# Attention and MLP in one kernel: q and k loads in a fixed chain of alternating halves, with a new order of all engines

## The chip, the cores and the metric

The kernel runs on one core of a Trainium2 chip. The metric is the device time of one execution in microseconds. Three runs of the kernel before took 606.34, 609.26 and 610.11 us, median 609.26 us.

## The reference

Causal attention over 4 batches, 12 heads, 448 tokens and a head size of 64, and then a feed-forward layer (768 to 2048 to 768) on the 1792 tokens that come out, all in float32:

```python
scores = (1.0 / np.sqrt(D)) * np.matmul(q, k.transpose(0, 1, 3, 2))
scores = np.where(np.triu(np.ones((S, S), dtype=bool), k=1), -1e9, scores)
attn = np.exp(scores - np.max(scores, axis=-1, keepdims=True))
attn = attn / (np.sum(attn, axis=-1, keepdims=True) + 1e-09)
x = np.matmul(attn, v).transpose(0, 2, 1, 3).reshape(B * S, H * D)
h = x @ w_in
g = np.where(h >= 1, h, np.where(h <= -1, 0.0, (h + 1) ** 2 / 4.0))
out = g @ w_out
```

## The kernel before, in words

**The work.** Two heads of a batch make a pair; there are 24. For a pair, q and k (two heads each) are loaded into `sq`, and DVE turns each into `qs` with a stream transpose (L736). PE makes the scores `s` (L838, in four PSUM buffers, all of which one pair fills), DVE adds the mask and takes the row minimum `mn` (L857, one instruction per tile of 64 to 448 columns and one that reads the minimum), ACT takes the exponential `e` with its row sum `su` (L861), the sum's reciprocal comes from DVE (L872), and `e` is scaled by it on POOL, ACT or DVE (L770, L772, L773). PE transposes `e` into `t` (L786), ACT or DVE copies it to `pt` (L809, L814), and PE multiplies it with v (`vr`) into `t` (L886). The result goes to `x` as a high and a low part (L470 or L471, and L479).

The first layer (`h`, L612) runs between the pairs' steps: for one batch and one block of 128 of the 2048 columns, six blocks of x by three passes (high by high, high by low, low by high), 18 matmuls. There are 64 such groups and two `h` buffers. Behind each group: `r = relu(h/2 + 1/2)` on ACT (L622), `vv = max(h, r)` on DVE (L625), and the clipped product `r = min(r, 1) * vv`, which is one instruction on DVE (L631) or two on POOL (L628, L629). `r` is stored to DRAM. There are three `r` buffers and one `vv` buffer. The weights of the first layer come as 384 KB loads into `w` and are decoded into a high and a low part in steps: ACT (L499, a Prelu into `wn`), DVE twice (L502, L504), then a copy (L470, L471) and a subtraction (L479 on DVE, L480 on POOL). There are four `wn` buffers. The weights of the second layer are decoded in the same way, combined by subtractions of `wn` to seven blocks per pair of rows, and kept in DRAM (`w_scratch`); the second layer (L1002) runs after all pairs, from about 400 us on.

**What sets the order.** The kernel lists tasks with the instructions that do them, what they read and write, and for some the engines that may do them. The class `Plan` puts them in order: it runs through a model of the engines and takes the next task by a rank. The tuple `STEPS` holds numbers, each of which seeds one random change of ranks or of the preferred engine (`shake`); the tuple therefore decides the order on all engines and who does what where there is a choice. A task that is `behind` another may not be put ahead of it in that order, but does not wait for its end. On the chip each engine works off its own list, and waits where a semaphore says so. All loads are issued by SP (L462).

**The loads of q and k.** `prep_pair` makes them. Pair 0 has two DMAs per tensor. Of the other 23 pairs each tensor (46 in all) has four DMAs of 32 partitions by 864 numbers (108 KB): head i and half z of the rows go to the partitions from `64 * i + 32 * z` on. Only the first of the four is `behind` something: the first load of the tensor before. The other three may be put anywhere after that, among other loads too. The transpose on DVE reads all four.

In the code, a program's names for buffers are those above. [rows n] in the prediction names the group of rows printed ahead of it.

Of the kernel before, what the change touches and what calls it, by code (L numbers as in the profile page):

```python
# [49 lines left out]
class Plan:  # L50
# [24 lines left out]
    def task(self, alts, prio, reads=(), writes=(), after=(), behind=()):  # L75
        t = Task([(*a, False) if len(a) == 3 else a for a in alts], prio)
        for b, k in reads:
            w, rs = b.keys.setdefault(k, [None, []])
            if w is not None:
                t.deps.add(w)  # L80
            rs.append(t)
        for b, k in writes:
            w, rs = b.keys.setdefault(k, [None, []])
            if w is not None:
                t.deps.add(w)
            t.deps.update(r for r in rs if r is not t)
            b.keys[k] = [t, []]
        for b in {id(x): x for x, _ in (*reads, *writes)}.values():
            if not b.tasks and b.tag is not None:
                t.allocs.append(b)  # L90
            elif b.tasks and b.tag is not None:
                t.soft.add(b.tasks[0])
            b.tasks.append(t)
        t.deps.update(after)
        t.soft.update(behind)
        t.deps.discard(t)
        t.soft -= t.deps
        for d in t.deps | t.soft:
            d.next.append(t)
        t.no = len(self.tasks)  # L100
        self.tasks.append(t)
        return t
# [47 lines left out]
    def solve(self):  # L150
# [23 lines left out]
        return self.run()  # L174

    STEPS = (
# [9 lines left out]
    )  # L186

    def shake(self, seed):
# [142 lines left out]
def mm(n, m=128, rows=128, times=1, pair=False):  # L331


    return [(n, m, rows, pair)] * times


def dve(n, fast=False):
    return ((n / 2 if fast else n) + 62) / 960


def act(n, extra=0.0):
    return n / 1200 + 0.055 + extra
# [10 lines left out]
def dma(nbytes, rate=250.0):  # L353
    return nbytes / rate / 1000
# [3 lines left out]
def kernel(  # L358
# [10 lines left out]
    B, H, S, D = q.shape  # L369
# [11 lines left out]
    C = S // 32  # L381
# [11 lines left out]
    LIGHT = 1  # L393
# [64 lines left out]
    def buf(tag, shape, dtype=F32):  # L458
        return plan.buf(tag, lambda: pools[tag].tile(shape, dtype, tag=tag, name=tag))

    def dma_task(out_fn, in_fn, cost, issue, early=False, lat=1.6, **kw):
        alts = [("SP", issue, lambda: nc.sync.dma_start(out=out_fn(), in_=in_fn())),  # L462
                ("ACT", issue, lambda: nc.scalar.dma_start(out=out_fn(), in_=in_fn()))]
        t = task(alts if early else alts[:1], 0.0, **kw)
        t.moved, t.lat = cost, lat
        return t
# [63 lines left out]
    ROW = C * D - 32  # L530
# [158 lines left out]
    attn_tasks, g_tasks, loads = [], [], []  # L689
# [5 lines left out]
    def tokens(t):  # L695
        return t[:, :NJ * 2 * D].rearrange("p (j g d) -> p j g d", g=2, d=D)

    def prep_pair(b, p, prio):
        no = b * HP + p
        x = QS[b, p] = [head[2 + g] if no == 0 else buf("qs", [P, S]) for g in range(2)]  # L700
        nat = []
        for g in range(2):
            t = head[g] if no == 1 else buf("sq", [P, ROW])
            first = None
            for i in range(2):
                row = (q, k)[g][b, 2 * p + i]
                if no < LIGHT:
                    one = dma_task(lambda i=i, t=t: tokens(t)[:, :, i],
                                   lambda row=row: bass.AP(row.tensor, row.offset, [[D, P], [P * D, NJ], [1, D]]),
                                   dma(NJ * P * D * 4, 228.0), 0.5, lat=1.45, early=no == 0, writes=[(t, i)],  # L710
                                   behind=loads[-1:] if first is None else ())
                    first = first or one
                    continue
                for z in range(2):
                    a = 64 * i + 32 * z
                    one = dma_task(lambda a=a, t=t: t[a:a + 32],
                             lambda row=row, z=z: bass.AP(row.tensor, row.offset + 32 * z, [[C * D, 32], [1, ROW]]),
                             dma(32 * 2 * S * 4, 230.0), 0.465, lat=1.25, writes=[(t, 2 * i + z)], behind=loads[-1:] if first is None else ())
                    first = first or one
            loads.append(first)  # L720
            nat.append(t)
        for g, t in enumerate(nat):
            if no < LIGHT:
                tb = buf("h" if no in (1, 2) or (no, g) == (0, 0) else "t", [P, 512])

                def tr(t=t, tb=tb):
                    for j in range(NJ):
                        n = min(P, S - j * P)
                        nc.tensor.transpose(tb[:, j * P:j * P + n], tokens(t)[:n, j].rearrange("p g d -> p (g d)"), ident[:n, :n])

                task([("PE", mm(215, 110, P, NJ), tr)], prio, reads=[(t, 0), (t, 1)], writes=[(tb, 0)]).nom = at(no, "S", 6) - LEAD + 0.1 * g
                task([("ACT", act(S, 0.04), lambda g=g, tb=tb: nc.scalar.activation(out=x[g].tile, in_=tb[:, :S], func=ACTF.Copy)),
                      ("DVE", dve(S), lambda g=g, tb=tb: nc.vector.tensor_copy(out=x[g].tile, in_=tb[:, :S]))],
                     prio, reads=[(tb, 0)], writes=[(x[g], 0)])
                continue
            task([("DVE", 0.81, lambda g=g, t=t: nc.vector.transpose(  # L736
                out=x[g].tile.rearrange("p (r c) -> p c r", c=C),
                in_=bands(t[:, :32])))],
                prio, reads=[(t, n) for n in range(4)], writes=[(x[g], 0)])
# [341 lines left out]
```

## Time and profile before

| | |
|---|---|
| runs | 606.34, 609.26, 610.11 us (median 609.26) |
| profiled execution | 608.45 us |
| its span | 606.7 us (1.75 us lie around it) |
| mean granted TensorE clock | 0.997 |
| PE busy | 588.1 us (97% of the span) |
| DVE, ACT, POOL busy | 454.0, 318.0, 147.5 us (75, 52, 24%) |

The profile is one execution. PE is the matrix engine, DVE the vector engine, ACT the scalar engine, POOL is GpSimd, SP issues the DMAs. A row of a timeline gives the start and the duration in us, the engine, the line of the kernel, the operation, what it writes and reads, the tile and the count; a bracket gives how long the engine stood idle before it, and what ended that. The granted clock is 1.00 at full speed (2.4 GHz) and 0.50 at the lower level (1.2 GHz). A float32 matmul shows as two in the trace where the kernel issues one in the scores and PV.

### The profile page before, as it was taken

How to read it: one execution, taken by the hardware profiler on the slowest of the kernel's cores; microseconds unless marked ns; L12 is line 12 of the kernel's file. 1: busy time of each engine (PE TensorE's matmuls, PEld its weight loads, DVE VectorE, ACT ScalarE, POOL GpSimd, SP SyncE). 2: the span in 40 equal slices, each digit the busy share in tenths (PEclk: the TensorE clock that was granted, in tenths of full speed). 3: DMA queues.
4: the chain of work that ended last, by engine and by line, in shares of the span. 5: the costliest groups of instructions: out<-in, count | busy, mean ns of one | idle time of the engine just before them, and what ended most of it. 6: DMA issues, size and time to landing. Idle time of an engine off the chain costs nothing.

```text
span 606.7 us, 11566 instructions
## 1 busy us (share of the span) xinstructions
PE 588.1 (97%) x3801; PEld 515.4 (85%) x3801; DVE 454.0 (75%) x1183; ACT 318.0 (52%) x811; POOL 147.5 (24%) x238
## 2 busy tenths in 40 slices
PE   8899799999999999999998999999999999999997
PEld 6566689877697887698796879999999999999997
DVE  4997888998876969966866559999766665566654
ACT  3999675888653655863665546845222232122220
POOL 2443444432133121442133303130000003200210
PEclk9999899999999999999999999999999999999999
DMA  8889898587778867597654339955324232433331
GB/s 198 242 210 244 239 287 251 157 225 219 216 207 260 255 229 227 157 286 246 183 180 134 126 102 327 350 153 169 122 70 128 83 121 60 133 95 101 112 93 54
DMA packets 98316, 109.97 MB, mean 181 GB/s; under 512 B 35536, under 2 KB 88272, under 8 KB 98256
## 3 DMA queue, kind: packets, MB, share of 16 engines
q1 hardware_dynamic: 97200, 108.97, 59.7%
q8 instruction: 30, 0.49, 0.3%
q10 hardware_dynamic: 1056, 0.26, 0.2%
q14 instruction: 30, 0.25, 0.1%
HBM read 78.00 MB, written 31.20 MB: 180 GB/s over the span
## 4 chain that ended last, share of the span: by engine, by line
PE 77%; DVE 11%; ACT 5%; DMA 2%; issue 2%; POOL 1%; SPq 0%; DVEq 0%; ACTq 0%
PE h L612 24%; PE s L1002 17%; PE h L1002 8%; PE s L612 8%; PE t L1002 8%; DVE s L857 4%; PE t L786 4%; PE t L886 4%; ACT e L861 3%; PE s L838 2%; DVE qs L736 2%; DMA vr<-in_v_dram 1%; PE h L912 1%; DVE wn L504 1%; DVE mn L857 1%
## 5 line engine op out<-in xcount | busy, mean ns | idle before, releaser
L612 PE MATMUL h<-x,w 128*128 128x448 f32 x900 | 204.6, 374 | 4.9 <-DVE vv L625 4.3
L612 PEld LDWEIGHTS h<-x,w 128*128 128x128 f32 x900 | 163.6, 190 | 18.8 <-DVE vv L625 5.5
L470 ACT ACTIVATE hl<-z 128x896 fp32r<-128x896 f32 x51 | 48.5, 952 | 127.8 <-DVE z L479 92.8
L1002 PE MATMUL s<-w,hl 128*128 128x384 f32 x552 | 104.7, 335 | 0.8 <-DVE vv L625 0.8
L1002 PEld LDWEIGHTS s<-w,hl 128*128 128x128 f32 x552 | 96.6, 188 | 1.1 <-DVE vv L625 1.1
L479 DVE TENSOR_TENSOR hl<-z,hl 128x896 fp32r<-128x896 f32 x54 | 60.4, 1119 | 49.2 <-ACT hl L470 43.8
L861 ACT ACTIVATE e<-s,mn 128x320 f32<-128x320 f32 (+6 forms) x168 | 78.0, 479 | 30.0 <-DVE mn L857 24.9
L857 DVE CUSTOM_DVE_ANT_0 s<-s,mask 128x320 f32<-128x320 f32 (+6 forms) x168 | 67.8, 447 | 6.7 <-PE s L838 4.2
L786 PE MATMUL t<-ident,e 128*128 128x128 f32 (+1 forms) x384 | 58.3, 277 | 5.5 <-ACT e L772 2.6
L786 PEld LDWEIGHTS t<-ident,e 128*128 128x128 f32 (+1 forms) x384 | 44.1, 139 | 16.9 <-ACT e L772 3.4
L479 DVE TENSOR_TENSOR z<-z 128x128 f32<-128x128 f32 x198 | 51.7, 292 | 5.7 <-DMA z<-g_scratch 2.4
L1002 PE MATMUL h<-w,hl 128*128 128x384 f32 x270 | 55.4, 335 | 0.0
L1002 PE MATMUL t<-w,hl 128*128 128x384 f32 x270 | 55.2, 335 | 0.0
L622 ACT ACTIVATE r<-h,half 128x448 f32<-128x448 f32 x50 | 31.5, 634 | 44.5 <-PE h L612 44.0
L770 POOL TENSOR_SCALAR e<-e,su 128x448 f32<-128x448 f32 (+6 forms) x74 | 42.9, 584 | 44.1 <-DVE su L872 36.7
L612 PE MATMUL s<-x,w 128*128 128x448 f32 x252 | 52.1, 363 | 0.0
L886 PE MATMUL t<-pt,vr 128*64 128x448 f32 (+3 forms) x384 | 49.8, 391 | 1.8 <-ACT pt L809 1.7
L625 DVE TENSOR_TENSOR vv<-h,r 128x448 f32<-128x448 f32 x50 | 31.0, 621 | 25.8 <-ACT r L622 22.9
L886 PEld LDWEIGHTS t<-pt,vr 128*64 128x64 f32 (+1 forms) x384 | 23.3, 135 | 31.0 <-issue 19.6
L612 PEld LDWEIGHTS s<-x,w 128*128 128x128 f32 x252 | 47.0, 188 | 3.1
L809 ACT ACTIVATE pt<-t 128x384 f32<-128x384 f32 (+2 forms) x94 | 44.3, 492 | 9.6 <-PE t L786 9.5
L1002 PEld LDWEIGHTS t<-w,hl 128*128 128x128 f32 x270 | 47.6, 188 | 0.0
(87 smaller groups left out, 753.9 us busy)
## 6 DMA issues: line engine op xcount, KB each, us to landing
g_scratch<-r SPq DMA_DIRECT2D x64, 224.0 KB, 3.2
z<-g_scratch SPq DMA_DIRECT2D x56, 256.0 KB, 2.8
sr<-in_moe_w_out_dram SPq DMA_DIRECT2D x32, 384.0 KB, 4.4
w<-in_moe_w_in_dram SPq DMA_DIRECT2D x28, 384.0 KB, 5.0
w_scratch<-wn SPq DMA_DIRECT2D x56, 192.0 KB, 3.6
w<-w_scratch SPq DMA_DIRECT2D x52, 192.0 KB, 4.3
sq<-in_q_dram SPq DMA_DIRECT2D x88, 108.0 KB, 2.8
sq<-in_k_dram SPq DMA_DIRECT2D x88, 108.0 KB, 2.8
```

What stands on the lines that cost most here:

```text
L470: "ACT": ("ACT", act(n, 0.04), lambda: nc.scalar.activation(out=dst(), in_=src(), func=ACTF.Copy)),
L479: "DVE": ("DVE", dve(n), lambda: nc.vector.tensor_tensor(out=dst(), in0=x(), in1=y(), op=op), port),
L612: nc.tensor.matmul(out=h[:, :S], lhsT=wi[f][kk // K2][:, a, kk % K2 * P:(kk % K2 + 1) * P], rhs=x[:, c], start=(kk == 0 and n == 0), stop= ...
L622: task([("ACT", act(S, 0.1), lambda: nc.scalar.activation(out=r.tile, in_=h[:, :S], func=ACTF.Relu, scale=0.5, bias=half[:, 0:1]))], g0, r ...
L625: task([("DVE", dve(S), lambda: nc.vector.tensor_tensor(out=y.tile, in0=h[:, :S], in1=r.tile, op=ALU.max))], g0, reads=[(h, 0), (r, 0)], w ...
L770: ("POOL", pool_ts(n, 0.09), lambda: nc.gpsimd.tensor_scalar(out=ev(), in0=ev(), scalar1=sc(), scalar2=1.0, op0=ALU.mult, op1=ALU.mult), T ...
L786: nc.tensor.transpose(t[:k, c:c + P], es[i][:, j * P:j * P + k], turners[i in SWAPPED])
L809: nc.scalar.activation(out=dst(), in_=src(), func=ACTF.Copy)
L857: task([("DVE", dve(n) + (0.05 if n < 384 else 0.02), lambda s=s, off=off, n=n, i=i: nc.vector.tensor_tensor_reduce(out=s[:, off:off + n], ...
L861: task([("ACT", act(n, 0.19), lambda s=s, off=off, n=n, i=i: nc.scalar.activation(out=es[i][:, :n], in_=s[:, off:off + n], func=ACTF.Exp, ...
L886: nc.tensor.matmul(out=o[64 * g:64 * g + 64, j * P:S], lhsT=vr[:k, j, g, :], rhs=pt[:k, 7 * j:5 * j + NI, g, :] if j < NJ - 1 else pt[:k, ...
L1002: nc.tensor.matmul(out=acc[x][:, :NO], lhsT=hl[:, a, i * P:(i + 1) * P], rhs=(hi, lo)[c](), start=(f == 0 and n == 0), stop=(f == KF - 2 a ...
```

## The change

The four loads of a tensor get a fixed order and a chain. The loop now goes over (z, i) = (0,0), (0,1), (1,0), (1,1), that is over the partitions 0, 64, 32, 96, so that consecutive loads go to different halves of the 128 partitions. Each load is `behind` the one before it, and the first of a tensor is behind the last of the tensor before. And `STEPS` is another tuple, with 139 numbers for 90, so that the order of all engines is another one.

```diff
     STEPS = (
-        5000008, 5000011, 5000014, 5000017, 5000022, 5000033, 5000036, 5000051, 5000059, 5000060, 5000097,
...
+        6000023, 6000032, 6000049, 6000062, 6000065, 6000069, 6000076, 6000082, 6000085, 6000091, 6000095,
...
     )
@@ prep_pair
             first = None
-            for i in range(2):
-                row = (q, k)[g][b, 2 * p + i]
-                if no < LIGHT:
+            if no < LIGHT:
+                for i in range(2):
+                    row = (q, k)[g][b, 2 * p + i]
                     one = dma_task(lambda i=i, t=t: tokens(t)[:, :, i],
...
                     first = first or one
-                    continue
-                for z in range(2):
+            else:
+                for z, i in ((0, 0), (0, 1), (1, 0), (1, 1)):
+                    row = (q, k)[g][b, 2 * p + i]
                     a = 64 * i + 32 * z
                     one = dma_task(lambda a=a, t=t: t[a:a + 32],
-                             lambda row=row, z=z: bass.AP(row.tensor, row.offset + 32 * z, [[C * D, 32], [1, ROW]]),
-                             dma(32 * 2 * S * 4, 230.0), 0.465, lat=1.25, writes=[(t, 2 * i + z)], behind=loads[-1:] if first is None else ())
+                                   lambda row=row, z=z: bass.AP(row.tensor, row.offset + 32 * z, [[C * D, 32], [1, ROW]]),
+                                   dma(32 * 2 * S * 4, 230.0), 0.465, lat=1.25, writes=[(t, 2 * i + z)], behind=loads[-1:] if first is None else [one])
                     first = first or one
+                first = one
             loads.append(first)
```

In the program that results, all 46 tensors go 0, 64, 32, 96. Before, 25 went 0, 32, 64, 96; 7 went 0, 64, 96, 32; 4 each 0, 96, 32, 64 and 0, 32, 96, 64; 3 each 0, 64, 32, 96 and 0, 96, 64, 32. PE and SP issue as many instructions as before. Some work changes its engine: `r` is on POOL 21 times for 8 and on DVE 43 for 56; subtractions of `wn` are on POOL 16 times for 3 and on DVE 18 for 31; the addition to the sums `su` is on DVE 27 times for 7; scalings of `e` move from POOL to DVE and ACT.

Lines of the changed kernel are 4 to 6 higher: L502 becomes L506, L504 L508, L625 L629, L631 L635, L628 and L629 L632 and L633, L736 L742, L857 L863, L861 L867.

On SP, at the loads of pairs 8 and 9, each row being one DMA or several of a kind in a row, stands before:

```order
L462 DMA w<-in_moe_w_in_dram 128x3x256 x3
L462 DMA sq<-in_q_dram 32x864 x2
L462 DMA w<-in_moe_w_in_dram 128x3x256
L462 DMA vr<-in_v_dram 128x4x64 x2
L462 DMA sq<-in_q_dram 32x864 x2
L462 DMA sq<-in_k_dram 32x864 x3
L462 DMA vr<-in_v_dram 128x4x64 x2
L462 DMA sq<-in_k_dram 32x864
L462 DMA sq<-in_q_dram 32x864 x2
L462 DMA sq<-in_k_dram 32x864 x4
L462 DMA w<-in_moe_w_in_dram 128x3x256
```

and now:

```order
L466 DMA w<-in_moe_w_in_dram 128x3x256 x4
L466 DMA sq<-in_q_dram 32x864
L466 DMA vr<-in_v_dram 128x4x64 x2
L466 DMA sq<-in_q_dram 32x864 x3
L466 DMA sq<-in_k_dram 32x864 x3
L466 DMA vr<-in_v_dram 128x4x64 x2
L466 DMA sq<-in_k_dram 32x864
L466 DMA sq<-in_q_dram 32x864 x4
L466 DMA sq<-in_k_dram 32x864 x4
L466 DMA w<-in_moe_w_in_dram 128x3x256
```

The fourth weight load has moved ahead of q, and the fifth stands behind four loads of q and four of k where it stood behind two and four.

On DVE, from the transposes of the next pair's q and k (`qs`) to the first mask of pair 7 (`ISA s`, the line of the masks), which is at 58 to 64 us in the trace before, stands before:

```order
L736 STREAM_TRANSPOSE qs_965<-sq_831 128x14x32
L479 TENSOR_TENSOR w_962<-wn_852,w_962 128x384
L872 RECIPROCAL su_909<-su_909 128x2
L869 TENSOR_SCALAR su_909<-su_909 128x3
L872 RECIPROCAL su_909<-su_909 128x3
L479 TENSOR_TENSOR x_989<-t_952,x_989 128x448
L502 TENSOR_SCALAR wn_879<-wn_879 128x384
L502 TENSOR_SCALAR wn_900<-wn_900 128x384
L504 SCALAR_TENSOR_TENSOR wn_879<-w_402,wn_879 128x384
L504 SCALAR_TENSOR_TENSOR wn_900<-w_418,wn_900 128x384
L471 CAST w_1032<-wn_879 128x384
L857 ISA s_996,mn_1039<-s_996,mask_116 128x448
```

and now, from the end of the masks of the pair before on:

```order
L506 TENSOR_SCALAR wn_865<-wn_865 128x384
L779 TENSOR_SCALAR e6_133<-e6_133,su_906 128x448
L508 SCALAR_TENSOR_TENSOR wn_865<-w_233,wn_865 128x384
L506 TENSOR_SCALAR wn_898<-wn_898 128x384
L475 CAST w_964<-wn_865 128x384
L742 STREAM_TRANSPOSE qs_967<-sq_740 128x14x32
L878 RECIPROCAL su_906<-su_906 128x2
L483 TENSOR_TENSOR w_964<-wn_865,w_964 128x384
L878 RECIPROCAL su_906<-su_906 128x3
L483 TENSOR_TENSOR x_981<-t_946,x_981 128x448
L863 ISA s_986,mn_1013<-s_986,mask_116 128x448
```

Before, a decode step, the transpose of q, a reciprocal and a copy stand ahead of the first row shown; now there is one transpose (q's) ahead of the mask, and k's stands 28 rows further on.

On ACT, at the same place, stands before:

```order
L809 ACTIVATE pt_984<-t_983 128x3x128
L811 ACTIVATE pt_984<-t_983 64x128
L499 ACTIVATE wn_1026<-w_232 128x384
L470 ACTIVATE w_1034<-wn_900 128x384
L622 ACTIVATE r_1043<-h_545,half_134 128x448
L622 ACTIVATE r_1055<-h_673,half_134 128x448
```

and now:

```order
L503 ACTIVATE wn_1016<-w_434 128x384
L867 ACTIVATE e6_133,su_1020<-s_986,mn_1013 128x448
L815 ACTIVATE pt_973<-t_972 128x3x128
L817 ACTIVATE pt_973<-t_972 64x128
L626 ACTIVATE r_1037<-h_543,half_134 128x448
L626 ACTIVATE r_1048<-h_681,half_134 128x448
L474 ACTIVATE w_1053<-wn_970 128x384
L867 ACTIVATE e5_132,su_1020<-s_987,mn_1013 128x384
L503 ACTIVATE wn_1063<-w_233 128x384
```

The two `r` stood behind the decode of the fifth weight load (`w_232`); now they stand ahead of it (`w_233`).

On DVE, later, where two groups of the first layer end beside the masks of a pair, stands before:

```order
L625 TENSOR_TENSOR vv_2806<-h_2682,r_2795 128x448
L631 SCALAR_TENSOR_TENSOR r_2795<-r_2795,vv_2806 128x448
L625 TENSOR_TENSOR vv_2832<-h_2691,r_2817 128x448
L857 ISA s_2809,mn_2835<-s_2809,mask_116 128x448
L857 ISA mn_2835 128x1
L631 SCALAR_TENSOR_TENSOR r_2817<-r_2817,vv_2832 128x448
```

and now:

```order
L629 TENSOR_TENSOR vv_2807<-h_2685,r_2793 128x448
L863 ISA s_2809,mn_2831<-s_2809,mask_116 128x448
L863 ISA mn_2831 128x1
L863 ISA s_2810,mn_2831<-s_2810,mask_116 128x384
L863 ISA mn_2831 128x1
L629 TENSOR_TENSOR vv_2842<-h_2693,r_2817 128x448
```

The two `r` have gone from DVE to POOL's list, and the second `vv` stands among the masks.

## Rows read from the trace of the kernel before

**Rows 1.** Busy time by stretch: us, PE, PEld, DVE, ACT, POOL, PEclk, DMA share, GB/s.

```profile
0.00:400.00 400.00, 385.67 (x2637) 313.58 (x2638) 315.72 (x876) 264.80 (x747) 127.89 (x206) 1.00 0.74 221
400.00:607.00 207.00, 202.48 (x1166) 201.84 (x1164) 138.24 (x308) 53.19 (x65) 19.61 (x33) 1.00 0.34 105
```

**Rows 2.** Timeline of PE: start, us, instruction, idle before and what ended it.

```profile
67.40 4.86 PE L612 MATMUL h<-x,w 128*128 128x448 f32 x15 [3.03 <-DVE vv L625]
...
127.33 0.55 PE L786 MATMUL t<-ident,e 128*128 128x128 f32 x3 [0.43 <-DVE x L479]
...
163.86 1.48 PE L612 MATMUL h<-x,w 128*128 128x448 f32 x6 [1.25 <-DVE vv L625]
...
330.02 0.66 PE L786 MATMUL t<-ident,e 128*128 128x128 f32 x4 [1.72 <-ACT e L772]
...
402.07 1.14 PE L1002 MATMUL s<-w,hl 128*128 128x384 f32 x5 [0.76 <-DVE vv L625]
```

**Rows 3.** Busy time by stretch around the largest wait of PE.

```profile
64.40:67.40 3.00, 0.00 (x1) 0.00 (x1) 1.67 (x6) 2.19 (x5) 1.95 (x2) 1.00 0.82 202
67.40:72.30 4.90, 4.90 (x17) 4.42 (x18) 4.27 (x17) 4.07 (x12) 2.46 (x4) 0.65 1.03 312
```

**Rows 4.** Chain of waits from 76 to 84 us: start, us, what.

```profile
76.11 3.01 PE h L612 x15
```

**Rows 5.** Timeline of DVE from 52 to 72 us.

```profile
56.23 0.56 DVE L504 SCALAR_TENSOR_TENSOR wn<-w,wn 128x384 uint32<-128x384 uint32 x1
57.40 0.95 DVE L736 STREAM_TRANSPOSE qs<-sq 128x448 f32<-128x448 f32 x1 [0.62 <-DMA sq<-in_k_dram]
...
60.19 0.96 DVE L736 STREAM_TRANSPOSE qs<-sq 128x448 f32<-128x448 f32 x1 [1.61 <-issue]
...
63.00 1.01 DVE L504 SCALAR_TENSOR_TENSOR wn<-w,wn 128x384 uint32<-128x384 uint32 x2
...
64.20 0.62 DVE L857 CUSTOM_DVE_ANT_0 s<-s,mask 128x448 f32<-128x448 f32 x1
...
66.72 0.62 DVE L625 TENSOR_TENSOR vv<-h,r 128x448 f32<-128x448 f32 x1 [1.33 <-ACT r L622]
```

**Rows 6.** Timeline of ACT from 58 to 70 us.

```profile
65.21 0.55 ACT L499 ACTIVATE wn<-w 128x384 f32<-128x384 f32 x1 [2.00 <-DMA w<-in_moe_w_in_dram]
...
66.07 1.14 ACT L622 ACTIVATE r<-h,half 128x448 f32<-128x448 f32 x2
```

**Rows 7.** Four loads of in_q_dram issued from 7.8 to 9.3 us (pair 2).

```profile
DMA to landing us min/median/max: 2.8/2.9/3.1
```

**Rows 8.** Four loads of in_k_dram issued from 9.7 to 11.1 us (pair 2).

```profile
DMA to landing us min/median/max: 2.8/2.8/3.1
```

**Rows 9.** Groups of instructions by line and form: busy us, mean ns, idle before.

```profile
L814 DVE COPY pt<-t 128x384 f32<-128x384 f32 x13 | 7.2, 554 | 1.8 <-PE t L786 1.8
```

**Rows 10.** Timeline of PE at scores of two pairs close together.

```profile
9.84 1.75 PE L838 MATMUL s<-x 64*64 64x448 f32 x28 [0.63 <-ACT x L732]
...
13.34 1.48 PE L838 MATMUL s<-qs 64*64 64x448 f32 x12
...
151.73 1.75 PE L838 MATMUL s<-qs 64*64 64x448 f32 x28
153.41 4.07 PE L886 MATMUL t<-pt,vr 128*64 128x448 f32 x30
157.22 0.59 PE L838 MATMUL s<-qs 64*64 64x448 f32 x2
```

**Rows 11.** Groups of instructions: r on POOL.

```profile
L628 POOL TENSOR_SCALAR r<-r 128x448 f32<-128x448 f32 x8 | 14.5, 1807 | 31.6 <-DVE vv L625 20.2 <-DMA w_scratch<-wn 10.7 <-DMA sq<-in_q_dram 0.6
...
L629 POOL TENSOR_TENSOR r<-r,vv 128x448 f32<-128x448 f32 x8 | 9.6, 1200 | 0.7
```

**Rows 12.** Timeline of DVE from 316 to 330 us.

```profile
322.80 0.62 DVE L625 TENSOR_TENSOR vv<-h,r 128x448 f32<-128x448 f32 x1 [2.19 <-POOL r L629]
```

**Rows 13.** All instructions of line 631: duration ns min/median/max, first and last start.

```profile
L631 DVE SCALAR_TENSOR_TENSOR r<-r,vv x56: 598/620/2548, 67.7 to 402.4; 128x448 f32<-128x448 f32 x56
```

20 rows, old and new, of the table STEPS are left out of this document.

## The prediction, made before the changed kernel was run

> **What bounds the kernel now.** The first view is the table by stretches [rows 1], cut at 400 us, where the pairs of heads and the first layer end. Look at PE's busy time: 385.67 of the first 400 us and 202.48 of the last 207. The granted clock is 1.00 in both, so there is no slow stretch to win back over a whole stage. PE is the bound, and a change of order that adds no matmul can only win what PE stands idle: 14.33 us and 4.52 us, 18.85 us in all. The other columns say who has room: DVE is busy 315.72 of the 400 us (79%), POOL 127.89 (32%).
>
> The second view is PE's timeline, read for the brackets behind its rows [rows 2]. The largest wait of the middle is 3.03 us at 67.40, for vv, the maximum that DVE takes of h and r. From 127.33 to 402.07 there are seven more waits, the first of 0.43 and the last of 0.76, and they add up to 6.2 us; the two largest are 1.25 at 163.86 and 1.72 at 330.02. The rest lies at the head and the tail, where the order of the loads decides little.
>
> The third view is the clock around the largest wait [rows 3]. PE does nothing from 64.40 to 67.40, and in the 4.9 us behind it the granted clock is 0.65, a mixture of the two levels. Its price stands in rows: 15 matmuls of the first layer take 4.86 us at 67.40 [rows 2] and 3.01 us when the clock is full [rows 4], so 1.85 us. In the other waits, up to 1.72 us, the clock stayed.
>
> So one place, 57 to 72 us, costs 3.03 + 1.85 = 4.9 us, and what ended last there is read from DVE and ACT [rows 5, 6]. The masks of pair 6 are through when the decode step at 56.23 begins. Then DVE holds two transposes of the next pair's q and k: it waits 0.62 us ahead of the first, for a load of k, and 1.61 us ahead of the second, for which the row names only issue (what can have come then is the quarter of k that SP issues last, behind two loads of v), and only at 64.20 do pair 7's masks begin. ACT holds the decode of a weight tile, which waits 2.00 us for its load, and the two r are behind it: they begin at 66.07 [rows 6]. vv follows at 66.72 and PE at 67.40. Two roads, through DVE and through ACT, thus end within about 1.4 us of each other, and both have to get shorter.
>
> **The change, part by part.** *Halves in turn.* All 46 tensors loaded in quarters now go to partitions 0, 64, 32, 96; before, the planner picked, and 3 of the 46 had just that order (25 went 0, 32, 64, 96). The number of DMAs and their bytes are as they were. At the head, where no backlog hides a transfer, the trace has both orders: pair 2's q went 0, 64, 32, 96 and landed 2.9 us (median) after its issue [rows 7], pair 2's k went 0, 32, 64, 96 and landed after 2.8 [rows 8]. So the alternation is worth 0, with 0.1 either way on any load that is on the path. The chain itself costs no wait on the chip: it is an order of issue on SP, where these DMAs stood in a row anyway.
>
> *The loads near 57 us.* The fifth weight load of that place is now issued two loads later, but r no longer stands behind its decode: the two r are ahead of it on ACT, behind one exp and one copy of pt. That shortens ACT's road. On DVE, before takes 64.20 - 56.23 = 7.97 us from the end of pair 6's masks to pair 7's, 2.23 of it in the two waits. After has one transpose instead of two, and it is the one of q (0.96 us less, and I count both waits as gone, since k's transpose now stands 28 rows behind q's instead of 3); it has the decode's third step once instead of three times (1.01 less [rows 5]); one scaling of e (0.54, taken as a 384 wide copy of pt [rows 9], which is the nearest row) replaces some short rows. I count those as even. Against that, two copies of pt now stand among pair 6's masks (2 x 0.55 [rows 9] = 1.1), and I take one row more ahead of them (0.55; nothing if the scores set their start, 1.1 if two do). Pair 7's masks then begin at 64.20 - 2.23 - 0.96 - 1.01 + 1.1 + 0.55 = 61.65. vv stands behind two masks as before (0.6 each), and besides behind four rows more, a mask and three decode steps of about 0.5: 61.65 + 1.2 + 1.9 = 64.7, so it ends at 65.3 and PE starts near 65.3 instead of 67.40. The wait goes from 3.03 to about 0.95: **-2.1 us**. And as no other wait up to 1.72 us brought the clock down, the fall goes too: **-1.85 us**. Bounds: nothing gained (both roads as late as before), or the whole 4.9.
>
> *Scores of two pairs close together.* In after PE does a pair's 14 score matmuls (28 in the trace, which counts both passes), one pair's PV, 6 score matmuls of the next pair, 4 transposes and that pair's last 8. The four score buffers are all taken by one pair, so the second must wait until DVE and ACT have emptied them, and by the rows it comes 1.75 and half of 4.07 = 3.8 us after the first began. In before the closest such two are 157.22 - 151.73 = 5.5 us apart and did not wait; at the head 13.34 - 9.84 = 3.5 us, without a wait as well, but there DVE had nothing else to do [rows 10]. So it costs between 0 and 5.5 - 3.8 = 1.7; I take **+0.7**, nearer to the head's rows.
>
> *r to POOL.* The clipped product r runs on POOL 21 times instead of 8, as two instructions of 1807 and 1200 ns instead of one of 620 on DVE [rows 11, 13]. POOL has the room; the price is elsewhere. There is one vv buffer, so the next vv on DVE waits until POOL has read the last one: at 322.80 DVE stood 2.19 us for this [rows 12], the masks queued behind it were late, and PE's 1.72 us at 330.02 came of it. Counting from the order the places where a vv follows one that POOL holds with less than 1.1 us of DVE work between them: 2 before, 9 after. With masks right behind it: 1 before, 4 after. So three more places can cost PE up to 1.72 each, 5.2 in all, or nothing where PE has other work. Before had two such places, and one of them cost PE something; half is the value taken: **+2.6**.
>
> What speaks further against this part is in the spread of r on DVE. Its median is 620 ns, and one took 2548 [rows 13]: a DVE instruction can be held by about 1.9 us. The Trainium skill ("SBUF — State Buffer", section "SBUF: two separate sides") says that DVE operations with two inputs in SBUF and GpSimd's share a port pair as an exclusive lock, the loser blocking for the whole instruction; the trace agrees with the single 2548, though a median close to the least, 598, shows that it is rare. By that rule the thirteen new pairs on POOL would hold DVE up to 13 x 1.93 = 25 us (an estimate), out of 84 idle in the first 400, and the last term would stand at its upper bound, the sum at 610.4; no chance changes by it, since the forecast's own range reaches that far.
>
> Thirteen subtractions of wn that go to POOL, the sums and scalings between POOL and DVE, and the copies of pt given to DVE I cost at nothing: DVE's 21% and POOL's 68% of idle time cover them, and where cover fails it shows as the waits above.
>
> **The sum**, against the profiled execution (608.45 us: the span of 606.7 and 1.75 around it; 0.13% under the median of 609.26): 608.45 - 2.1 - 1.85 + 0.7 + 2.6 = **607.8 us**.
>
> **The rivals.**
> B, the order also closes other waits. For it: 13 r off DVE free 13 x 0.62 = 8 us of it, the subtractions some more, and three of the four middle waits in [rows 2] end with DVE. Against: the largest, 1.72, ends with ACT's e. If the POOL places cost nothing and half of the 6.2 us goes: 608.45 - 3.95 - 3.1 = 601.4; with none of it gone 604.5. I put it at 603.0.
> C, slower: the one vv buffer decides. Its place is every stretch in which POOL does r twice in a row, five in a row at one of them. A vv cannot come sooner than 0.62 + 1.81 + 1.20 and some hand-overs, about 3.9 us, after the last, while PE gives a group of 18 matmuls in 18/15 x 3.01 = 3.6 [rows 4]. From the point where h's two buffers no longer cover this, all nine places cost, seven more than before at 1.72: 608.45 - 3.95 + 0.7 + 12.0 = 617.2. Against: one of before's two places cost nothing.
> D, the change does not do what it says at 57 us: DVE's or ACT's road is as late as it was, for a load two places later or for the four rows more ahead of vv. Then 608.45 + 0.7 + 2.6 = 611.8.
>
> **How the numbers follow.** Forecast 0.45, B 0.25, C 0.15, D 0.15. One per cent, about what a measurement of this kernel can tell from no change, is 6.1 us off the median: below 603.2 counts as faster, above 615.4 as slower. Faster holds a bit over half of B and a little of the forecast, 0.2; slower holds C and a little of D, 0.17; same the rest, 0.63. The range from 601.5 to 614 leaves out most of C and the end of B. The forecast's own range is 604.5 (r on POOL and the close scores free) to 610.4 (r on POOL at its upper bound).
>
> **What would show it.** Right: PE's wait near 65 us is under 1.5 us with the clock at full speed behind it; pair 7's masks begin by 62; q and k land 2.8 to 2.9 us after issue at the head; DVE waits for POOL's r at several vv, and behind some of them PE waits one to two us. Wrong: a wait of 3 us or a fall of the clock anywhere in the middle; a load that lands later or sooner by the new order; no vv that waits for POOL; or more PE idle time than 18.85 us without POOL in its chain.

## The result, and the profile after

The changed kernel is slower. Nine runs of each on the same chip gave a median of 612.14 us (609.99 to 614.72) against 607.57 us (605.90 to 610.11), ratio 1.007, interval 1.0044 to 1.0095. The forecast was 607.8, a little faster than before. The time lies inside the range, but on the other side of the kernel before, and clearly so. The profiled execution took 612.23 us, its span is 610.1.

The table by stretches of the changed kernel, which answers to [rows 1], and its two stretches that answer to [rows 3]:

```profile
0.00:400.00 400.00, 383.36 (x2615) 308.56 (x2616) 314.40 (x895) 262.35 (x736) 152.55 (x199) 1.00 0.73 219
400.00:611.00 211.00, 206.50 (x1188) 205.72 (x1186) 140.73 (x308) 51.56 (x64) 32.59 (x44) 1.00 0.35 106
...
64.40:67.40 3.00, 3.00 (x17) 2.49 (x17) 2.96 (x14) 2.36 (x8) 2.24 (x3) 1.00 0.85 289
67.40:72.30 4.90, 4.37 (x27) 3.71 (x26) 4.90 (x10) 4.19 (x11) 3.50 (x3) 1.00 0.52 151
```

The fall of the clock at 67 us is gone: 64.4 to 67.4 us is busy through, at 1.00. In the first 400 us PE is busy 2.3 us less than before (383.36 against 385.67). Some 1.6 of these are the busy time that the slow clock had added; the rest is work that has moved behind 400 us. POOL is busy 24.7 us more. The timeline of PE (answers to [rows 2 and 10]) shows where PE now stands:

```profile
64.15 2.68 PE L616 MATMUL h<-x,w 128*128 128x448 f32 x12 [0.70 <-DVE vv L629]
...
156.86 1.32 PE L844 MATMUL s<-qs 64*64 64x256 f32 x16 [0.16 <-ACT e L867]
...
204.28 0.44 PE L792 MATMUL t<-ident,e 128*128 128x128 f32 x2 [1.61 <-ACT e L778]
210.78 5.08 PE L616 MATMUL h<-x,w 128*128 128x448 f32 x24 [0.71 <-DVE vv L629]
216.96 0.98 PE L792 MATMUL t<-ident,e 128*128 128x128 f32 x7 [1.09 <-ACT e L778]
238.77 0.98 PE L792 MATMUL t<-ident,e 128*128 128x128 f32 x7 [0.82 <-ACT e L778]
```

The wait of 3.03 us has become 0.70. From 175 to 300 us there are 11 waits now, 7.43 us in all, where before had two, 1.39 us. That stretch is most of the loss: by the starts of the same numbered vv, the changed kernel is 3.2 us ahead at the first group, 0.5 ahead at the 25th (192.47 against 192.96), 6.4 behind at the 41st (293.78 against 287.35) and 3.5 behind at the 64th, the last. These steps are rough, because what PE does between two groups is in another order too; where the 2.7 us between the first and the 25th went is not followed.

The waits by engine, of DVE and then of PE, in the changed kernel (us, times, longest) name the engine behind it:

```profile
DVE vv L629 <- ACT r L626: 22.4, 18, 4.2
DVE vv L629 <- POOL r L633: 16.0, 8, 3.1
...
PE h L616 <- DVE vv L629: 5.5, 10, 1.2
PE t L792 <- ACT e L778: 4.1, 4, 1.6
```

vv waits for POOL's r 8 times, 16.0 us in all; before it was once, 2.2 us [rows 12]. One such place is the one whose order is shown ahead of the prediction, `vv_2807` and `vv_2842`. DVE and POOL there, in the changed kernel:

```profile
206.41 0.61 DVE L629 TENSOR_TENSOR vv<-h,r 128x448 f32<-128x448 f32 x1
...
210.10 0.62 DVE L629 TENSOR_TENSOR vv<-h,r 128x448 f32<-128x448 f32 x1 [0.97 <-POOL r L633]
...
213.99 0.95 DVE L875 TENSOR_SCALAR su<-su 128x2 f32<-128x2 f32 x1
215.28 0.17 DVE L878 RECIPROCAL su<-su 128x3 f32<-128x3 f32 x1 [0.34 <-POOL su L873]
```

```profile
207.11 1.72 POOL L632 TENSOR_SCALAR r<-r 128x448 f32<-128x448 f32 x1 [4.67 <-DVE vv L629]
208.91 1.16 POOL L633 TENSOR_TENSOR r<-r,vv 128x448 f32<-128x448 f32 x1
210.03 0.99 POOL L484 TENSOR_TENSOR wn<-wn 128x384 f32<-128x384 f32 x1
210.99 1.70 POOL L632 TENSOR_SCALAR r<-r 128x448 f32<-128x448 f32 x1
212.78 1.17 POOL L633 TENSOR_TENSOR r<-r,vv 128x448 f32<-128x448 f32 x1
213.91 1.01 POOL L484 TENSOR_TENSOR wn<-wn 128x384 f32<-128x384 f32 x1
215.00 0.25 POOL L873 TENSOR_SCALAR su<-su 128x3 f32<-128x3 f32 x1
```

Three things are to be seen. The second vv waits until POOL has read the first. The addition to su, 0.25 us long, comes at 215.00 because two r and two subtractions of wn stand ahead of it in POOL's list; its reciprocal follows at 215.28, ACT's e, and PE at 216.96. And the addition to su that DVE does at 213.99 takes 0.95 us, where the median of its kind is 0.157: it ends with POOL's subtraction.

### The profile page after: what moved, and what is told of

The parts are those of the page before. It is cut to its first block, busy times and chain, and to the rows that moved or that the text cites. A ratio compares the mean times of both kernels' runs of the same rounds, so it can differ in the third digit from the quotient of the medians.

```text
span 610.1 us, 11572 instructions
## 1 busy us (share of the span) xinstructions
PE 589.9 (97%) x3801; PEld 514.3 (84%) x3801; DVE 455.1 (75%) x1203; ACT 313.9 (51%) x800; POOL 185.1 (30%) x242
## 4 chain that ended last, share of the span: by engine, by line
PE 46%; DMA 8%; DVE 5%; POOL 2%; issue 2%; ACT 2%; SPq 1%; DVEq 0%; ACTq 0%; POOLq 0%
PE s L1008 17%; PE h L1008 8%; PE t L1008 8%; PE h L616 6%; DMA w<-w_scratch 4%; DMA sr<-in_moe_w_out_dram 2%; PE t L792 2%; PE t L892 2%; PE s L616 1%; PE s L844 1%; POOL r L632 1%; DMA w_scratch<-wn 1%; DMA g_scratch<-r 1%; DVE vv L629 1%; SPq L466 1%
## 5 line engine op out<-in xcount | busy, mean ns | idle before, releaser
L474 ACT ACTIVATE hl<-z 128x896 fp32r<-128x896 f32 x46 | 43.8, 952 | 125.4 <-DVE z L483 96.3
L867 ACT ACTIVATE e<-s,mn 128x128 f32<-128x128 f32 (+6 forms) x168 | 77.9, 477 | 27.6 <-DVE mn L863 24.4
L483 DVE TENSOR_TENSOR hl<-z,hl 128x896 fp32r<-128x896 f32 x54 | 58.8, 1089 | 44.2 <-ACT hl L474 35.5
L863 DVE CUSTOM_DVE_ANT_0 s<-s,mask 128x320 f32<-128x320 f32 (+6 forms) x168 | 67.7, 446 | 7.5 <-PE s L844 5.4
L483 DVE TENSOR_TENSOR z<-z 128x128 f32<-128x128 f32 x193 | 56.1, 319 | 7.6 <-DMA z<-g_scratch 3.5
L484 POOL TENSOR_TENSOR z<-z 128x128 f32<-128x128 f32 x31 | 18.0, 582 | 134.7 <-DVE z L483 114.2
L629 DVE TENSOR_TENSOR vv<-h,r 128x448 f32<-128x448 f32 x50 | 31.0, 620 | 36.1 <-ACT r L626 19.6
L632 POOL TENSOR_SCALAR r<-r 128x448 f32<-128x448 f32 x21 | 36.7, 1746 | 42.7 <-DVE vv L629 38.6
L1008 PEld LDWEIGHTS h<-w,hl 128*128 128x128 f32 x270 | 47.6, 188 | 0.0
```

The source lines that it names most:

```text
L474: "ACT": ("ACT", act(n, 0.04), lambda: nc.scalar.activation(out=dst(), in_=src(), func=ACTF.Copy)),
L483: "DVE": ("DVE", dve(n), lambda: nc.vector.tensor_tensor(out=dst(), in0=x(), in1=y(), op=op), port),
L484: "POOL": ("POOL", pool_tt(n), lambda: nc.gpsimd.tensor_tensor(out=dst(), in0=x(), in1=y(), op=op), True),
L629: task([("DVE", dve(S), lambda: nc.vector.tensor_tensor(out=y.tile, in0=h[:, :S], in1=r.tile, op=ALU.max))], g0, reads=[(h, 0), (r, 0)], w ...
L632: nc.gpsimd.tensor_scalar(out=r.tile, in0=r.tile, scalar1=1.0, scalar2=1.0, op0=ALU.min, op1=ALU.mult)
L863: task([("DVE", dve(n) + (0.05 if n < 384 else 0.02), lambda s=s, off=off, n=n, i=i: nc.vector.tensor_tensor_reduce(out=s[:, off:off + n], ...
```

## The experiments

Theory 1 was that the loss is POOL's r, by way of the single vv buffer; rival 2, that the masks and e are late there for other reasons. Beside them stood the question what the loads' new order is worth by itself. All ratios are to the kernel before on the same chip; differences in us between two changed kernels are of medians from different chips.

**r on DVE** (after_r_dve). The list of every engine stays as it was, but for r.

```diff
-            nc.gpsimd.tensor_scalar(out=r.tile, in0=r.tile, scalar1=1.0, scalar2=1.0, op0=ALU.min, op1=ALU.mult)
-            nc.gpsimd.tensor_tensor(out=r.tile, in0=r.tile, in1=y.tile, op=ALU.mult)
+            nc.vector.scalar_tensor_tensor(
+                out=r.tile, in0=r.tile, scalar=1.0, in1=y.tile, op0=ALU.min, op1=ALU.mult)
```

> The changed kernel with all 21 of POOL's r done by DVE, at the same places of the order; all else as it was. Theory 1 (POOL's r behind the single vv buffer makes the loss between 193 and 290 us): DVE's 16.0 us of waiting for POOL's r go, DVE takes 21 x 0.62 = 13 us of work in their place, and PE's waits from 200 to 290 us fall from 6.8 to about 2 us: 607 us, ratio to before 0.995 to 1.001. Rival 2 (the masks and e are late there for other reasons: the loads of w_out, wn subtractions on POOL, su): the waits stay, 611 to 613 us.

Measured: 602.59 us, ratio 0.9922 (0.9895 to 0.9949). It beats both kernels; 9.5 us go, nearly twice what I expected. The stretch from 175 to 300 us (columns as in [rows 1]) of the kernel before, the changed kernel, and the changed kernel with r on DVE:

```profile
175.00:300.00 125.00, 123.35 (x844) 101.84 (x843) 98.08 (x263) 71.33 (x202) 36.27 (x56) 1.00 0.75 227
```

```profile
175.00:300.00 125.00, 117.53 (x795) 94.23 (x794) 86.01 (x252) 65.97 (x184) 59.48 (x55) 1.00 0.71 217
```

```profile
175.00:300.00 125.00, 123.43 (x857) 101.61 (x859) 99.08 (x284) 72.83 (x202) 16.11 (x27) 1.00 0.75 224
```

PE's busy time, the first number behind 125.00, falls from 123.35 to 117.53 and is back at 123.43 without POOL's r: some 5.9 of the 9.5 us are here.

**The reverse, on the kernel before** (before_r_pool): its order kept, with a list that puts r on POOL where the changed kernel has it.

```diff
+    R_ON = "DPDPDDDDDDDDDDDDDPDDPPPPPPPDPPDDPPPDPPDPDDDDDPDPDDDDDDDDDDDDDPDD"
...
+            (pool_g if R_ON[len(r_no) - 1] == "P" else on_dve)()
```

> The kernel before, its order kept, with r on the engine that the changed kernel has for the same number of group: 21 on POOL instead of 8. Theory 1: PE waits several more times between 175 and 295 us, 611 to 613 us, ratio about 1.008. Rival 2: within 1.5 us of the kernel before.

Measured: 625.15 us, ratio 1.0283 (1.0232 to 1.0333), more than three times the loss that was expected. In an order that was not made for it POOL's r costs more still; a part of the price is the clock, which in the profiled execution (granted clock 0.989) fell four times where before's fell once. With the 8 r that before has on POOL given to DVE (before_r_dve, the same edit as the first):

> The kernel before with its 8 r of POOL on DVE, order kept. If each r on POOL costs as in the changed kernel (9.5 us for 21): 8 x 0.45 = 3.6 us less, 603.5. If only the places where r comes twice in a row cost: 1 to 2 us less, 605.5. If nothing: 607.

Measured: 605.10 us, ratio 0.9946 (0.9920 to 0.9972), 3.1 us less. So the r on POOL had their price in the kernel before too, about 0.4 us each. That POOL's r is the cause stands, and rival 2 falls. Whether the single vv buffer is the way is the next question.

**By which road.** Two vv buffers, with the order unchanged (after_vv2):

```diff
-            pools[t] = stack.enter_context(tc.tile_pool(name=f"p_{t}", bufs=slots[t], **kw))
+            pools[t] = stack.enter_context(tc.tile_pool(name=f"p_{t}", bufs=slots[t] + (t == "vv"), **kw))
```

> The changed kernel with two vv buffers in memory instead of one, and the order as it was; POOL still does 21 r. If the hand-over of the one buffer is what costs: no vv waits for POOL's r, 607 to 608 us. If POOL's own time costs (DVE held while POOL works, r late for its store and so for the next r): 611 to 612 us.

Measured: 610.70 us, ratio 1.0049 (1.0024 to 1.0073). No vv waits for POOL any more, but only 1.4 us of the 9.5 come back. Then the opposite: r on DVE, and POOL does a pair of the same kind of instructions whose result in a spare tile nobody uses (after_spare_pair), or a tiny instruction and six memsets (after_spare_sets). The first instruction of the stand-in reads r, so that a later r on ACT can still wait for POOL: it did so once, 1.7 us, with the pair, and twice, 3.6 us, with the memsets.

```diff
+            nc.gpsimd.tensor_scalar(out=spare, in0=r.tile, scalar1=1.0, scalar2=1.0, op0=ALU.min, op1=ALU.mult)
+            nc.gpsimd.tensor_tensor(out=spare, in0=spare, in1=spare, op=ALU.mult)
...
```

```diff
+            nc.gpsimd.tensor_scalar(out=spare[:, :1], in0=r.tile[:, :1], scalar1=1.0, scalar2=1.0, op0=ALU.min, op1=ALU.mult)
+            for _ in range(6):
+                nc.gpsimd.memset(spare, 0.0)
...
```

> The changed kernel with r on DVE (as in the run that took 602.6 us), and behind each of the 21 r that POOL had, POOL does the same two instructions on a spare tile that nobody waits for (the first reads r, the second has both inputs in the spare tile). If POOL being busy is what costs (its own queue of e, su and wn subtractions is late, or DVE is held by it): 608 to 612 us. If r and vv being late costs: 602 to 604 us.

> As the run with the spare pair, but POOL's stand-in is one tiny instruction that reads a column of r and six memsets of the spare tile, some 3 us in all, which read nothing. If POOL's queue is what costs, the same time as with the pair. If DVE is held by POOL's instructions that read SBUF, less: near 603 us, and DVE's busy time about that of the run with r on DVE.

Measured: 610.02 us, ratio 1.0029 (1.0006 to 1.0051), with the pair; 611.18, ratio 1.0039 (1.0023 to 1.0056), with the memsets. A POOL that is busy with results nobody needs costs 7.4 us.

The clock hides a part of these differences. Of the nine runs of the changed kernel eight have a mean granted clock of 0.999 or more, and of the nine with r on DVE seven; with two vv buffers it is two of 12, with the pair five of 12, with the memsets none. Runs at that clock alone have medians of 611.93 (changed kernel), 602.22 (r on DVE), 608.24 (two vv buffers, two runs only) and 608.97 (pair). Compared so, the second vv buffer brings back 3.7 of 9.7 us, and the pair costs 6.8. The two roughly add up: by this estimate, from few runs, about a third of the price is the hand-over of vv, and two thirds are POOL's time. PE at the place shown above, in the changed kernel with two vv buffers and with the pair, and the stretch behind the pair's wait (columns as in [rows 1]):

```profile
214.44 0.98 PE L792 MATMUL t<-ident,e 128*128 128x128 f32 x7 [2.16 <-ACT e L778]
```

```profile
215.43 1.75 PE L797 MATMUL t<-ident,e 128*128 128x128 f32 x7 [2.76 <-ACT e L783]
```

```profile
215.40:218.70 3.30, 3.27 (x12) 3.06 (x13) 2.41 (x5) 0.99 (x2) 0.00 (x0) 0.50 0.84 264
```

What were three shorter waits in the changed kernel (1.61, 0.71 and 1.09) is one longer wait in these two, and behind the pair's the clock is 0.50: the seven transposes take 1.75 us where they took 0.98. The runs with two vv buffers that lost time to the clock left no trace, so that theirs fell at this place is not shown.

The busy times on the page of r on DVE, of the pair and of the memsets:

```profile
PE 586.8 (98%) x3801; PEld 514.9 (86%) x3801; DVE 458.9 (76%) x1224; ACT 313.7 (52%) x800; POOL 122.8 (20%) x200
```

```profile
PE 590.2 (97%) x3801; PEld 516.2 (85%) x3801; DVE 471.9 (78%) x1224; ACT 313.2 (52%) x800; POOL 179.4 (30%) x243
```

```profile
PE 589.9 (97%) x3801; PEld 516.9 (85%) x3801; DVE 464.3 (76%) x1224; ACT 313.6 (51%) x800; POOL 191.3 (31%) x348
```

DVE has the same 1224 instructions in all three, and takes 13.0 us longer for them beside the pair, 5.4 beside the memsets. That is the hold that the single 2548 ns showed [rows 13], now counted; a subtraction of 2.12 us on POOL had begun 0.05 us before that one. The Trainium skill ("SBUF — State Buffer", section "SBUF: two separate sides") has the exclusive lock of a port pair between DVE's operations with two SBUF inputs and GpSimd's that read SBUF, and between DVE's in a 2-port mode and any of GpSimd's; the runs agree, with 13.0 us of DVE for 21 pairs, and with less than half beside instructions that mostly only write; which mode DVE's were in, no trace shows. But the memsets cost PE as much, so DVE being held is not the whole of it: POOL's list is the other part. They are no clean test, though: they keep POOL busy 11.9 us longer than the pair does, and the clock fell twice in their profiled execution (0.994). The same place, DVE and POOL, with the spare pair:

```profile
213.75 0.18 DVE L883 RECIPROCAL su<-su 128x3 f32<-128x3 f32 x1 [1.29 <-POOL su L878]
```

```profile
211.50 0.93 POOL L638 TENSOR_TENSOR spare<-spare 128x448 f32<-128x448 f32 x1
212.40 0.99 POOL L487 TENSOR_TENSOR wn<-wn 128x384 f32<-128x384 f32 x1
213.47 0.25 POOL L878 TENSOR_SCALAR su<-su 128x3 f32<-128x3 f32 x1
```

Nothing uses the spare tile, and still the reciprocal waits 1.29 us for su, which stands behind it. With r on DVE and POOL free, the same reciprocal runs at 211.23 without a wait.

**What stands behind r.** Four more runs: su and wn on DVE with r on POOL (after_su_wn_dve), the same with two vv buffers (after_vv2_su_wn), two vv buffers and e on ACT (after_vv2_e_act), and r and wn on DVE (after_r_wn_dve). The edits put the other engine's instruction into the task's POOL entry, so that the order stays:

```diff
-                ("POOL", 0.315, lambda a=a, z=z: nc.gpsimd.tensor_scalar(
-                out=su[:, a:z], in0=su[:, a:z], scalar1=1e-9, scalar2=0.0, op0=ALU.add, op1=ALU.add), True),
+                ("POOL", 0.315, lambda a=a, z=z: nc.vector.tensor_scalar(
+                out=su[:, a:z], in0=su[:, a:z], scalar1=1e-9, scalar2=None, op0=ALU.add), True),
...
```

> The changed kernel with its 21 r on POOL, but POOL's su additions and wn subtractions on DVE, so that of what PE waits for only scalings of e are left behind r in POOL's list. If the loss is that su waits behind r and wn on POOL: 606 to 608 us. If it is vv's wait for POOL's r or the scalings of e: 611 to 613 us.

> The changed kernel with two vv buffers, and POOL's su additions and wn subtractions on DVE; r (21 times) and the scalings of e stay on POOL. With two vv buffers alone it took 610.7, with su and wn alone 616.2 (su then stood behind vv's that wait for POOL). If the two roads from POOL's r to PE are vv's hand-over and su behind r: both are gone, 603 to 606 us. If it is the scalings of e behind r, or DVE held while POOL works: 608 to 611.

> The changed kernel with two vv buffers, and POOL's 50 scalings of e on ACT; r, su and wn stay on POOL. If e behind r in POOL's list is the second road: 603 to 606 us. If it is su: 608 to 612, as with two vv buffers alone, or more where ACT gets late.

> The changed kernel with r and also the subtractions of wn on DVE. If POOL's list of short instructions (su, e) still waits behind subtractions of 1 us: 600 to 602 us. If r was all: 602.6. If DVE, with 16 x 0.58 = 9 us more, gets short: 604 or more.

Measured: su and wn on DVE 616.22 us, ratio 1.0132 (1.0097 to 1.0166); with two vv buffers 612.16, ratio 1.0064 (1.0039 to 1.0088); e on ACT 624.40, ratio 1.0254 (1.0221 to 1.0286); r and wn on DVE 603.58, ratio 0.9929 (0.9900 to 0.9957). The last says that r is all: the subtractions add nothing beside it. The other three missed: 606 to 608, 603 to 606 and 603 to 606 us were expected of them if su, su beside vv's hand-over, or e was the way, and none comes near 602.6. They do not settle it either, for each puts work on an engine ahead of what PE waits for; with su and wn on DVE and two vv buffers, the two subtractions of wn, 1.49 and 1.00 us long, stand on DVE around the second vv and ahead of su, and PE waits 1.00 and 1.01 us there.

So it is shown that r on POOL costs, that POOL's busy time costs the larger part of it and vv's hand-over the smaller. That su's position behind r does the damage is read from the trace at one place; the runs made to test it do not bear it out. How POOL's part divides between its list and DVE being held stays open.

**The loads.** The new loads with the old tuple of numbers (chain_old_steps); the lists of PE, DVE, ACT and POOL come out as before:

```diff
-        6000023, 6000032, 6000049, 6000062, 6000065, 6000069, 6000076, 6000082, 6000085, 6000091, 6000095,
...
+        5000008, 5000011, 5000014, 5000017, 5000022, 5000033, 5000036, 5000051, 5000059, 5000060, 5000097,
...
```

> The new loads (chain and alternating halves) with the old tuple of numbers: the lists of PE, DVE, ACT and POOL come out as before, only SP's list and the addresses of the loads change. If the chain does no more than the alternation: as the kernel before with its halves in turn, ratio 0.997 (605.5 to 607). If the chain itself makes loads late: 609 or more. Either way the changed kernel's loss then belongs to the new order.

Measured: 606.93 us, ratio 0.9990 (0.9960 to 1.0019). The loads are not the loss. The alternation alone was taken away twice and added once, by giving the n-th load issued for a tensor the n-th address of another list (its source in the same way):

```diff
+                    def dst(t=t, todo=todo, now=now):
+                        now[:] = todo.pop(0)
+                        a = 64 * now[1] + 32 * now[0]
+                        return t[a:a + 32]
...
```

> The changed kernel with every tensor's four loads at the same places of SP's list, but to partitions 0, 32, 64, 96 instead of 0, 64, 32, 96. If the alternation is worth nothing: 611.5 to 612.7 us, within 0.1% of the changed kernel. If alternating halves helps: 1 us or more slower; if it hurts, 1 us or more faster.

> The changed kernel with r on DVE (602.6 us) and the loads of a tensor to 0, 32, 64, 96 in SP's same places. If the alternation under a backlog is worth what the first pair of runs showed (614.7 against 612.1): 605. If that was chance: 602.6.

> The kernel before with each tensor's four loads at the same places of SP's list, but always to partitions 0, 64, 32, 96. If the alternation is worth nothing: within 0.2% of the kernel before. If it is worth what the run of the changed kernel without it suggests (614.7 against 612.1): 2 to 3 us less, 604.5, ratio 0.996.

Measured: the changed kernel without it 614.74 us, ratio 1.0127 (1.0089 to 1.0166); with r on DVE without it 603.61, ratio 0.9936 (0.9911 to 0.9961), against 602.59 with it; the kernel before with it 607.16 beside 608.19, ratio 0.9969 (0.9946 to 0.9991). All three point one way, by 1.0 to 2.6 us, and only the last is clear of its interval. The landing of the loads of q and then of k, over the whole of the changed kernel and over the whole of the same without the alternation:

```profile
DMA to landing us min/median/max: 2.2/3.1/7.3
...
DMA to landing us min/median/max: 2.2/3.1/6.2
```

```profile
DMA to landing us min/median/max: 2.3/3.7/7.1
...
DMA to landing us min/median/max: 2.1/3.6/5.7
```

The median landing is 0.5 to 0.6 us later without it. But the other pairs show less: with r on DVE it is 3.1 with the alternation and 3.6 without for q, 3.3 and 3.4 for k; in the kernel before 2.8 and 2.7 with it, 2.8 and 2.8 without. At the head the two orders were alike [rows 7, 8]. So how the alternation helps stays open.

## Why the prediction was wrong

**The place at 57 us: right, but for the price of the clock.** Pair 7's masks were to begin at 61.65, vv at 64.7, the wait to be 0.95 and the clock to stay. DVE's and ACT's timelines of the changed kernel, which answer to [rows 5, 6]:

```profile
60.81 0.62 DVE L863 CUSTOM_DVE_ANT_0 s<-s,mask 128x448 f32<-128x448 f32 x1
...
63.48 0.61 DVE L629 TENSOR_TENSOR vv<-h,r 128x448 f32<-128x448 f32 x1
```

```profile
62.67 1.15 ACT L626 ACTIVATE r<-h,half 128x448 f32<-128x448 f32 x2
```

Masks at 60.81, both r at 62.67 instead of 66.07, vv at 63.48, a wait of 0.70: 2.33 us gained for 2.1. Rival D is out. The fall of the clock is gone as well, with 1.00 behind the wait, and in eight of the nine runs the mean clock is 0.999 or more. Its price was read from two unlike rows: the 3.01 us at 76.11 is a part of the chain, which begins later than its matmuls. PE's timeline of the same trace has them in 3.25:

```profile
75.87 3.25 PE L612 MATMUL h<-x,w 128*128 128x448 f32 x15
```

So the fall cost 4.86 - 3.25 = 1.6 and not 1.85. And the profile shown of before is only the commoner of its cases: of its 20 runs beside the first experiments, 14 had a mean clock of 0.997 or less and six 0.999 or more, with medians of 607.8 and 605.75. So against the median run the term is nearly right, and against a third of the runs it is not there. That no wait up to 1.72 us brings the clock down held here, but other runs show that it need not (last section).

**Scores close together: right in kind, too large.** 0.7 was put; PE's wait at 156.86 is 0.16.

**Halves in turn: too small.** 0 was put, with 0.1 either way per load. It helps, by 1 to 2.6 us in three pairs of runs, not clear of the interval in two.

**r to POOL: the step that failed.** I counted nine places with a hand-over of vv, let only those cost that have masks right behind them, three more than before, and priced them at half of 1.72: +2.6, 5.2 at most. The count of the hand-overs held: 8 waits of DVE. What failed is that the hand-over was taken for the whole price. By the runs the 21 r on POOL cost 9.5 us and the 8 of before 3.1, so the change's share is 6.4 (an estimate from two orders, some 3 us either way by the intervals of the ratios), where 2.6 was put and 5.2 was the upper bound. Two vv buffers give back 1.4 of the 9.5, or 3.7 of 9.7 at the full clock; the rest is POOL's time itself, which I had covered with "POOL has the room" and POOL's 68% of idle time. An average does not tell of the moment at which su or e stands behind 3 us of r. The rule of the Trainium skill that I weighed and set at my upper bound spoke for this; 25 us of held DVE was put as its limit for 13 pairs, and 13.0 were found beside 21.

With the measured terms the sum is 608.45 - 2.33 - 1.6 + 0.16 + 6.4 = 611.1, and with the 1 to 2.6 us that the halves in turn gave, 608.5 to 610.1, against 612.23 of the profiled execution. So 2 to 4 us are in none of the terms, though the uncertainty of the 6.4 alone could hold most of that. Rival C had the right place and the right sign; its 12.0 us, one 1.72 for each place, were about twice too many, and the one vv buffer, which it took for the whole mechanism, is the smaller part. "No fall of the clock", "pair 7's masks by 62" and "DVE waits for POOL's r at several vv" came true; of PE's waits of one to two us that stretch has two. PE's idle time is 20.2 us (span less busy time), above the 18.85 that was set as a sign of being wrong without POOL in the chain; here POOL is in it.

## What to carry to other kernels

An engine that is idle two thirds of the time is not free: price the long instructions that are given to it by the short ones behind them in its list, for which the bound engine waits, and by what it holds on the engine that shares its way to the memory. A stand-in whose result nobody uses tells the cost of an engine's time apart from the cost of a late result in one run, if it is compared at the same granted clock: a test that draws several short waits together can lose by the clock what it gains by the wait. And where the order of everything is searched anew, look at what changed its engine, not only at the places that the change names: here the alternation was worth 1 to 2.6 us, the new order won 4 at one place, and gave back more with 13 products that had moved.

## What the runs showed of the hardware

A wait of PE does not always bring the clock down. In the kernel before with its halves in turn, PE stood almost as long as at 67.40 [rows 2], and 15 matmuls then ran in 3.29 us and not in 4.86:

```profile
66.66 3.29 PE L612 MATMUL h<-x,w 128*128 128x448 f32 x15 [2.73 <-DVE vv L625]
```

In other runs it came down behind shorter ones: in the kernel before with r on POOL the clock was 0.50 from 213.2 to 216.5 us, behind a wait of 2.06, and from 278.0 to 281.4, a little after a wait of 1.56 (the matmuls in the middle of these rows):

```profile
213.06 0.66 PE L796 MATMUL t<-ident,e 128*128 128x128 f32 x2 [2.06 <-ACT pt L819]
213.37 2.59 PE L615 MATMUL h<-x,w 128*128 128x448 f32 x6
...
276.42 0.66 PE L796 MATMUL t<-ident,e 128*128 128x128 f32 x4 [1.56 <-POOL e L780]
```

Six matmuls of the first layer took 2.59 us there, and 1.48 at the full clock. So the length of a wait alone does not tell whether the clock falls, and a forecast of it is in part luck.

DVE took 13.0 us longer for the same 1224 instructions when POOL did 21 pairs whose results nobody used. One-input instructions were held too: the addition to su took 0.95 us, for a median of 0.157, while POOL did a subtraction.
